# One scatter a unit for tiles 6 to 19, and folds dealt to units without low halves of rows or the transform alone

## The chip, the cores and the metric

The kernel runs on one core of a Trainium2 chip. Its time is the device time of one launch in microseconds (us). The page of the profile names five engines: PE (TensorE, with PEld for its weight loads), DVE (VectorE), ACT (ScalarE), POOL (GpSimd) and SP (SyncE, which here only issues DMAs).

## The reference

```python
X = fft(fft(x, axis=1), axis=2).real          # x: 8 x 3072 x 256
a = x @ w_a; b = x @ w_b                      # x is now 24576 x 256, w_a and w_b 256 x 1536
x = (a * b) @ w_out                           # back to 24576 x 256
e_idx = argmax(x @ w_gate)                    # one of 8 experts for each row
out[row] = gate_w * eom * (relu(x[row] @ w1[e]) @ w2[e])
```

All matrix products run in float16 with each factor split into a high and a low half, and three of the four products of halves summed.

## The kernel before

**Stages.** A batch's x is first folded: the symmetric parts of its rows are added and subtracted, in six pieces c of 128 rows (`fold_items`, L498). A piece takes `fold1` (L515, three POOL instructions) and `fold2` (L524, four, and two more for c above 2). Then the folded x is scaled and split into halves (`hi`, `lo`, L592 to L600), the transform along the sequence is taken with matmuls against tables that are loaded from HBM (`dft_products`, L650), and the two matrices w_a and w_b, already turned by the transform along the feature axis, are applied (`step`, L850).

**Units.** The middle of the program is a list of 327 units (`plan`, L1187), run in order. A unit "B" is one block of 128 of the 1536 inner features for one tile of 1024 rows (24 tiles, three to a batch, 12 units a tile): 12 matmuls of 128x512 (L828), the product a*b on DVE (L834 to L840 and L861), its high half on ACT (L845), its low half on POOL (L847), and two units later 24 matmuls of 128x256 with w_out (`g2`, L888). A unit "D" is one twelfth of the transform for a group of batches, with no block of features beside it; each of the groups 1 to 4 (`GROUPS`, L34) begins with nine of them, and its last three twelfths ride in "B" units.

**After a tile.** `post_items` (L901) takes the 1024 rows that a tile made: their squares, the high halves on ACT (`row_hi`), the low halves on DVE (`row_lo`, L947, one instruction for 128 rows, in units of 2, 3 and 3), eight transposing DMAs (`turn`), the gates (`gate0` to `gate3`, some 15 small DVE instructions), the place of each row in its expert's list (`place`), and eight indirect DMAs (`scatter`, L1048 to L1050), each of which writes 128 rows to the table `rows` in HBM from POOL's queue. A scatter waits until the scatter before it has landed, since both write `rows`. Beside this run the folds of later batches and `expert_items` (L368), which split the experts' weights, with low halves on DVE (`lo1` L412, `lo2` L465).

**Who sets the order.** `deal` (L185) gives each list of items to units: an item goes to the first unit whose `BUDGET` of ACT, DVE, POOL and SP time it still fits. `reserve` (L182) books room. In a unit, `second` (L842) issues ACT's high half, then what the planner put under "pool0", then POOL's low half L847, and after it `run("pool")`; DVE's items come behind L840. Items of `post_items` are dealt first, then those of the folds and of the experts. All engines then work through their queues in that order, waiting on semaphores.

After the units comes a drain, and then the experts' stage (from L1558 on, 83 blocks of 256 rows and 23 of 128), which sorts nothing any more and is bound by PE.

Of the kernel before, what the change touches and what calls it, by code (L numbers as in the profile page):

```python
# [41 lines left out]
def chain_kernel(ctx, tc, x, x384, w_a, w_b, w_out, w_gate, w_og, w1, w2, dft, c16, c32, ids, out):  # L42
# [129 lines left out]
    def run(point):  # L172
# [3 lines left out]
    BUDGET = {  # L176
        "B": {"act": 2.8, "dve": 1.75, "pool": 3.6, "pe": 1.0, "sp": 4.0},
        "D": {"act": 1.8, "dve": 1.8, "pool": 3.2, "pe": 1.0, "sp": 4.0},
    }
# [318 lines left out]
    def fold_items(b, eng):  # L498
# [25 lines left out]
        def fold2(c):  # L524
            def go():
# [5 lines left out]
                eng.tensor_tensor(out=T if c > 2 else F32[:, c, 0, :], in0=A[:, 0, :], in1=A[:, 1, :], op=ALU.add)  # L531
                eng.tensor_tensor(out=F32[:, c, 1, :], in0=A[:, 0, :], in1=A[:, 1, :], op=ALU.subtract)
                if c > 2:
                    eng.tensor_tensor(out=F32[:, c, 0, :], in0=F32[:, c - 3, 0, :], in1=T, op=ALU.subtract)
                    eng.tensor_tensor(out=F32[:, c - 3, 0, :], in0=F32[:, c - 3, 0, :], in1=T, op=ALU.add)
            return go
# [68 lines left out]
        for i, c in enumerate(order):  # L605
            for k, fn in enumerate((fold1(c), fold2(c))):
                if i == 1 and k == 0:
                    t.append((0, [("sp", 1, load384)]))
                due = [norms.popleft()] if i > 3 and norms else []
                nx = [("sp", 1, load(order[i + 1]))] if k == 1 and i < 5 else []  # L610
                t.append((1 + (i == 0 and k == 0), [("pool", 2.1 if k == 0 else 3.6 if c > 2 else 2.2, fn)] + nx + due))
            if i == 1:
# [288 lines left out]
    def post_items(T):  # L901
# [161 lines left out]
        for a, b in ((0, 2), (2, 5), (5, 8)):  # L1063
            if a >= nt:
                continue
            m = min(b, nt) - a
            items.append((0 if last is None and nt > 4 else 1, [("act", 0.4 * m, c(row_hi, a, b)), ("dve", 0.38 * m, c(row_lo, a, b))] + ([("sp", 2, last)] if last else [])))
            last = c(turn, a, b)
# [6 lines left out]
        ]  # L1075
        for w in range(0, nt, 2):
            items.append((1, [("pool0", 1.3, scatter(w))] + ([("pool", 1.3, scatter(w + 1))] if w + 1 < nt else [])))
# [111 lines left out]
    for g, G in enumerate(GROUPS):  # L1189
        if g:  # L1190
            plan += [("D", g, i, i, 9) for i in range(9)]
            reserve(len(plan) - 1, "act", 0)
            reserve(len(plan) - 1, "dve", 0)
# [670 lines left out]
```

## Time and profile before

| | |
|---|---|
| time, median of 3 runs | 3057.61 us (3049.89 to 3060.44) |
| profiled execution | 3049.82 us, span 3048.1 us |
| PE busy in the span | 2873.9 us (94%) |
| DVE busy | 2212.1 us (73%) |
| POOL busy | 1335.4 us (44%) |
| mean granted PE clock | 0.978 |

The span is the time from the first to the last instruction. The window rows cover, in this order, tiles 7, 8, 9 and 10, the start of tile 11, tiles 14, 15 and 16, three units in tile 17, tiles 20 and 21, and the "D" units of groups 3 and 4 with the unit before them. A share of busy time is an average over stages: in the units DVE is nearly as full as PE, in the experts' stage PE alone is full. Times in windows are counted from the start of the span. "idle before" in a row is the time in which the engine did nothing just before, and the name behind the arrow is what ended it. The profiled execution lies at the lower end of the three runs.

### The profile page before, as it was taken

How to read it: one execution, taken by the hardware profiler on the slowest of the kernel's cores; microseconds unless marked ns; L12 is line 12 of the kernel's file. 1: busy time of each engine (PE TensorE's matmuls, PEld its weight loads, DVE VectorE, ACT ScalarE, POOL GpSimd, SP SyncE). 2: the span in 40 equal slices, each digit the busy share in tenths (PEclk: the TensorE clock that was granted, in tenths of full speed). 3: DMA queues.
4: the chain of work that ended last, by engine and by line, in shares of the span. 5: the costliest groups of instructions: out<-in, count | busy, mean ns of one | idle time of the engine just before them, and what ended most of it. 6: DMA issues, size and time to landing. Idle time of an engine off the chain costs nothing.

```text
span 3048.1 us, 62392 instructions
## 1 busy us (share of the span) xinstructions
PE 2873.9 (94%) x24101; PEld 2181.6 (72%) x24101; DVE 2212.1 (73%) x4079; ACT 1313.7 (43%) x2605; POOL 1335.4 (44%) x1083
## 2 busy tenths in 40 slices
PE   6899899989999989999989999989999999999998
PEld 3566666756666756666666666688888888888898
DVE  8678699688999688999677998744555555555556
ACT  4444455545455445455444444432333333333332
POOL 6466587365775455775333544413211111111112
PEclk7899999999999999999999999999999999999999
DMA  6321622541221551221352212373222222222211
GB/s 210 99 61 43 177 69 60 144 108 44 77 76 47 137 119 46 77 72 46 97 128 84 78 50 89 80 193 96 54 52 51 53 51 52 50 53 51 52 45 34
DMA packets 363577, 244.48 MB, mean 80 GB/s; under 512 B 303101, under 2 KB 320669, under 8 KB 362382
## 3 DMA queue, kind: packets, MB, share of 16 engines
q1 hardware_dynamic: 342158, 184.75, 24.3%
q0 software_dynamic: 18816, 51.54, 5.0%
q10 hardware_dynamic: 2304, 4.20, 0.5%
q8 instruction: 188, 3.08, 0.4%
q14 instruction: 111, 0.91, 0.1%
HBM read 106.60 MB, written 70.33 MB: 58 GB/s over the span
## 4 chain that ended last, share of the span: by engine, by line
PE 72%; DVE 13%; issue 7%; DMA 4%; ACT 3%; POOL 0%; DVEq 0%; SPq 0%; POOLq 0%; ACTq 0%
PE s L828 18%; PE y L894 17%; PE g L1611 16%; PE g L1635 15%; PE s L662 3%; DVE EE L861 2%; DVE s L837 2%; DVE rows L947 2%; DVE hf L840 1%; DVE AM L835 1%; DMA big<-in_dft_dram 1%; DMA rows<-rows,di 1%; PE s L962 1%; ACT BP L834 1%; ACT hl L845 1%
## 5 line engine op out<-in xcount | busy, mean ns | idle before, releaser
L828 PE MATMUL s<-big 128*128 128x512 f16 x3456 | 818.9, 387 | 77.0 <-DVE EE L861 69.2
L847 POOL TENSOR_TENSOR hl<-hf,hl 128x1024 f16<-128x1024 f32 x288 | 626.0, 2174 | 562.4 <-ACT hl L845 431.7
L894 PE MATMUL y<-big,hl 128*128 128x256 f16 x6912 | 820.9, 273 | 0.7 <-POOL hl L847 0.5
L894 PEld LDWEIGHTS <-hl 128*128 128x128 f16 x6912 | 672.1, 98 | 150.7 <-issue 10.7
L828 PEld LDWEIGHTS <-big 128*128 128x128 f16 x3456 | 342.7, 99 | 448.6 <-issue 115.6
L1638 POOL DMA_INDIRECT out_dram<-o,di x189 | 192.1, 1017 | 781.6 <-ACT o L1637 521.1
L845 ACT ACTIVATE hl<-hf 128x1024 f16<-128x1024 f32 x288 | 303.9, 1055 | 507.7 <-DVE hf L840 454.1
L1611 PE MATMUL g<-yt,w1t 128*128 128x256 f16 (+1 forms) x4704 | 493.9, 265 | 3.8 <-DVE w1t L1592 3.8
L1635 PE MATMUL g<-w2t,hh 128*128 128x256 f16 x2896 | 479.5, 273 | 0.0
L1611 PEld LDWEIGHTS <-w1t 128*128 128x128 f16 x4704 | 432.5, 98 | 50.9 <-DVE w1t L1592 4.1
L1614 DVE SCALAR_TENSOR_TENSOR hl<-g,hh 128x512 f16<-128x512 f32 x378 | 260.7, 691 | 241.8 <-ACT hh L1613 241.7
L1635 PE MATMUL g<-w2t,hl 128*128 128x256 f16 x1448 | 394.8, 273 | 0.0
L1613 ACT ACTIVATE hh<-g 128x512 f16<-128x512 f32 x378 | 225.3, 597 | 280.0 <-PE g L1611 280.0
L1635 PEld LDWEIGHTS <-hh 128*128 128x128 f16 x3024 | 294.8, 98 | 33.9
L1050 POOL DMA_INDIRECT rows<-rows,di x192 | 192.7, 1004 | 258.7 <-DMA rows<-rows,di 190.2
L836 DVE SCALAR_TENSOR_TENSOR hf<-s,BP 128x512 f32<-128x512 f32 x288 | 198.2, 688 | 109.1 <-ACT BP L834 99.3
L1596 DVE COPY w2t<-big 128x4104 f16 x98 | 120.4, 1229 | 207.9 <-PE g L1635 207.9
L1637 ACT ACTIVATE o<-g,sc 128x256 f32<-128x256 f32 x189 | 89.5, 473 | 406.3 <-PE g L1635 359.7
L835 DVE SCALAR_TENSOR_TENSOR AM<-EE,s 128x512 f32<-128x512 f32 x288 | 195.9, 680 | 29.9 <-PE s L828 27.7
L861 DVE SCALAR_TENSOR_TENSOR EE<-xe,w,s 128x512 f32<-128x512 f32 x288 | 201.4, 740 | 5.1 <-PE s L828 5.1
L861 DVE SCALAR_TENSOR_TENSOR EE<-big,w,s 128x512 f32<-128x512 f32 x288 | 201.5, 741 | 0.0
L837 DVE SCALAR_TENSOR_TENSOR s<-EE,s 128x512 f32<-128x512 f32 x288 | 197.1, 684 | 0.0
(332 smaller groups left out, 3012.4 us busy)
## 6 DMA issues: line engine op xcount, KB each, us to landing
big<-in_x_dram SPq DMA_DIRECT2D x48, 514.0 KB
big<-in_dft_dram SPq DMA_DIRECT2D x60, 384.0 KB
big<-in_moe_w_dram SPq DMA_DIRECT2D x16, 1024.0 KB
wsc<-big SPq DMA_DIRECT2D x32, 512.0 KB
big<-wsc SPq DMA_DIRECT2D x7, 2050.0 KB
big<-in_dft_dram SPq DMA_DIRECT2D x60, 192.0 KB
big<-wsc ACTq DMA_DIRECT2D x16, 256.2 KB
tail<-rows SPq DMA_TRANSPOSE x192
```

Source lines behind the costliest of these rows:

```text
L828: pe.matmul(out=s[ab], lhsT=Wt[:, ab, uv, a, fs], rhs=src[:, h + uv, :], start=(uv == 0 and i == 0), stop=(i == 2), skip_group_check=(uv = ...
L835: dve.scalar_tensor_tensor(out=AM[:, 0, :], in0=EE[:, 0, :], scalar=2.0, in1=a, op0=ALU.mult, op1=ALU.subtract)
L836: dve.scalar_tensor_tensor(out=P["hf"][:, 0, :], in0=a, scalar=CA * CA, in1=BP, op0=ALU.mult, op1=ALU.mult)
L837: dve.scalar_tensor_tensor(out=b, in0=EE[:, 1, :], scalar=2.0, in1=b, op0=ALU.mult, op1=ALU.subtract)
L845: act.activation(out=hl[:, 0], in_=hf, func=ACTF.Copy)
L847: pool.tensor_tensor(out=hl[:, 1], in0=hf, in1=hl[:, 0], op=ALU.subtract)
L861: dve.scalar_tensor_tensor(out=EE[:, ab, :], in0=st_x[T[0]], scalar=w0[:, ab, f:f + 1], in1=s[ab], op0=ALU.mult, op1=ALU.add)
L894: pe.matmul(out=Y[w // 2][:, w % 2, :], lhsT=hl[:, h, pm, 128 * j:128 * j + 128], rhs=wo[:, f, a, :], start=(f == 0 and i == 0 and w % 2 = ...
L1611: pe.matmul(out=ps[:, u, :], lhsT=w[:, a, q, 128 * f:128 * f + 128], rhs=yt[:, 2 * h + q, :], start=(m == 0), stop=(m == 5))
L1613: act.activation(out=hh[:, f0:f0 + nu, :], in_=ps, func=ACTF.Relu)
L1614: dve.scalar_tensor_tensor(out=hl[:, f0:f0 + nu, :], in0=ps, scalar=0.0, in1=hh[:, f0:f0 + nu, :], op0=ALU.max, op1=ALU.subtract)
L1635: pe.matmul(out=ps, lhsT=hx[:, f, ts], rhs=wv[:, a, f, :], start=(m == 0), stop=(m == 3 * NF2 - 1))
```

## The change

Three rules of the planner change, and `fold2` is split. No arithmetic changes. (a) Tiles 6 to 19 deal their eight scatters one to a unit, all under "pool0", where before two shared a unit, one ahead of L847 and one behind it. (b) A new resource "lock" with room 1.0 in each unit: the low halves of rows of tiles 6 and above take 1.0 of it, each part of a fold of batches 4 to 7 takes 0.5, and the nine "D" units of groups 2, 3 and 4 have it booked out. So these folds share no unit with low halves of rows, and neither stands in those "D" units; that also moves the low halves of tiles 11 and 17, which stood there. (c) For batches 4 to 7 the last two instructions of `fold2` become `fold3`, an item of its own, in the same unit where POOL's budget allows.

```diff
     BUDGET = {
-        "B": {"act": 2.8, "dve": 1.75, "pool": 3.6, "pe": 1.0, "sp": 4.0},
-        "D": {"act": 1.8, "dve": 1.8, "pool": 3.2, "pe": 1.0, "sp": 4.0},
+        "B": {"act": 2.8, "dve": 1.75, "pool": 3.6, "pe": 1.0, "sp": 4.0, "lock": 1.0},
+        "D": {"act": 1.8, "dve": 1.8, "pool": 3.2, "pe": 1.0, "sp": 4.0, "lock": 1.0},
...
+                st["T", c] = T
+            return go
+
+        def fold3(c):
+            def go():
+                T = st["T", c]
+                eng.tensor_tensor(out=F32[:, c, 0, :], in0=F32[:, c - 3, 0, :], in1=T, op=ALU.subtract)
+                eng.tensor_tensor(out=F32[:, c - 3, 0, :], in0=F32[:, c - 3, 0, :], in1=T, op=ALU.add)
+            return go
...
-            for k, fn in enumerate((fold1(c), fold2(c))):
+            for k, fn in enumerate((fold1(c), both(c)) if b < 4 else (fold1(c), fold2(c)) + ((fold3(c),) if c > 2 else ())):
...
-                t.append((1 + (i == 0 and k == 0), [("pool", 2.1 if k == 0 else 3.6 if c > 2 else 2.2, fn)] + nx + due))
+                t.append((int(k < 2) + (i == 0 and k == 0), [("pool", (2.1, 2.2 if c < 3 or b > 3 else 3.6, 1.35)[k], fn), ("lock", 0.5 if b > 3 else 0.0, None)] + nx + due))
...
-            items.append((0 if last is None and nt > 4 else 1, [("act", 0.4 * m, c(row_hi, a, b)), ("dve", 0.38 * m, c(row_lo, a, b))] + ([("sp", 2, last)] if last else [])))
+            items.append((0 if last is None and nt > 4 else 1, [("act", 0.4 * m, c(row_hi, a, b)), ("dve", 0.38 * m, c(row_lo, a, b)), ("lock", 1.0 if t > 5 else 0.0, None)] + ([("sp", 2, last)] if last else [])))
...
-        for w in range(0, nt, 2):
+        if 5 < t < NTILE - 4:
+            items += [(1, [("pool0", 1.3, scatter(w))]) for w in range(nt)]
+        for w in range(0, nt if not 5 < t < NTILE - 4 else 0, 2):
             items.append((1, [("pool0", 1.3, scatter(w))] + ([("pool", 1.3, scatter(w + 1))] if w + 1 < nt else [])))
...
             plan += [("D", g, i, i, 9) for i in range(9)]
+            if g > 1:
+                for u in range(len(plan) - 9, len(plan)):
+                    reserve(u, "lock", 1.0)
```

The first place is POOL's queue where tile 7's rows are scattered and tile 8's low halves stand on DVE (units 130 to 134 of the plan). L1050 is a scatter, L847 the low half of a unit's product, L529 to L532 are a `fold2`. Before:

```order
L1050 DMA rows<-rows_100,di 196864x264 x2
L847 TENSOR_TENSOR hl<-hf,hl 128x1024
L1050 DMA rows<-rows_100,di 196864x264
L847 TENSOR_TENSOR hl<-hf,hl 128x1024
L529 TENSOR_TENSOR big<-big 128x2x129
L530 TENSOR_TENSOR big<-big 128x2x127
L531 TENSOR_TENSOR big<-big 128x256
L532 TENSOR_TENSOR big<-big 128x256
```

These are the last three scatters of the tile; the pair at the top is the second scatter of one unit and the first of the next. The fold behind them stands in a unit with three low halves of rows.

With the change the first three scatters of the same tile read so (L1062 is the scatter, L859 the low half of a unit, L519 to L521 a `fold1`, L529 to L532 a `fold2`):

```order
L1062 DMA rows<-rows_100,di 196864x264
L859 TENSOR_TENSOR hl<-hf,hl 128x1024
L519 TENSOR_TENSOR big<-big 128x4x128
L520 TENSOR_TENSOR big<-big 128x4x127
L521 COPY big<-big 128x4
L1062 DMA rows<-rows_100,di 196864x264
L859 TENSOR_TENSOR hl<-hf,hl 128x1024
L529 TENSOR_TENSOR big<-big 128x2x129
L530 TENSOR_TENSOR big<-big 128x2x127
L531 TENSOR_TENSOR big<-big 128x256
L532 TENSOR_TENSOR big<-big 128x256
L1062 DMA rows<-rows_100,di 196864x264
```

No scatter follows another directly any more. In 16 units of the plan one scatter and one part of a fold now stand together; there were none before.

The second place is DVE's queue at the end of the "D" units of group 3. L691 is the low half of a twelfth of the transform, L947 the low halves of tile 11's rows. Before:

```order
L947 SCALAR_TENSOR_TENSOR rows_100<-tail,r_11610,rows_100 128x256 x2
L159 TENSOR_SCALAR pq<-sst 128x2
L160 TENSOR_SCALAR Rt<-pq 128x2
L691 SCALAR_TENSOR_TENSOR big<-s_115,Rt,big 128x256 x2
L159 TENSOR_SCALAR pq<-sst 128x2
L160 TENSOR_SCALAR Rt<-pq 128x2
L691 SCALAR_TENSOR_TENSOR big<-s_116,Rt,big 128x256 x2
L947 SCALAR_TENSOR_TENSOR rows_100<-tail,r_11610,rows_100 128x256 x3
```

All eight instructions of the tile stand in "D" units. With the change the first two come behind the first "B" unit's part of the transform (L703 is the old L691, L873 the old L861, L959 the old L947):

```order
L703 SCALAR_TENSOR_TENSOR big<-s_117,Rt,big 128x256 x2
L873 SCALAR_TENSOR_TENSOR EE<-xe,w_91,s_114 128x512
L873 SCALAR_TENSOR_TENSOR EE<-xe,w_91,s_115 128x512
L159 TENSOR_SCALAR pq<-sst 128x2
L160 TENSOR_SCALAR Rt<-pq 128x2
L703 SCALAR_TENSOR_TENSOR big<-y_118,Rt,big 128x256 x2
L959 SCALAR_TENSOR_TENSOR rows_100<-tail,r_11598,rows_100 128x256 x2
```

Its transposes, gates and scatters move back with it, by four to six units. The same happens to tile 17 in group 4.

## Rows read from the trace of the kernel before

**Rows 1.** The page's first part: each engine's busy us, share of the span, instructions.

```profile
PE 2873.9 (94%) x24101; PEld 2181.6 (72%) x24101; DVE 2212.1 (73%) x4079; ACT 1313.7 (43%) x2605; POOL 1335.4 (44%) x1083
```

**Rows 2.** Windows: start:end, length, busy us of PE, PEld, DVE, ACT, POOL; PEclk; DMA.

```profile
692.40:756.20 63.80, 63.80 (x480) 43.00 (x478) 55.08 (x112) 35.91 (x72) 35.50 (x26) 1.00 0.11 27
756.20:829.10 72.90, 66.55 (x495) 44.23 (x494) 68.23 (x121) 34.80 (x64) 50.42 (x41) 0.95 0.28 81
829.10:897.70 68.60, 66.05 (x498) 44.15 (x497) 63.90 (x119) 38.31 (x73) 56.39 (x50) 1.00 0.29 78
897.70:966.00 68.30, 65.25 (x498) 44.01 (x496) 63.04 (x128) 35.90 (x71) 34.11 (x21) 1.00 0.18 48
992.20:1015.20 23.00, 21.23 (x148) 14.28 (x147) 21.16 (x35) 7.47 (x11) 11.94 (x7) 1.00 0.52 139
1217.10:1289.20 72.10, 67.34 (x496) 44.47 (x494) 65.57 (x122) 34.92 (x64) 49.54 (x41) 0.95 0.29 82
1289.20:1359.10 69.90, 66.08 (x497) 44.01 (x495) 65.33 (x118) 38.20 (x73) 56.05 (x50) 1.00 0.28 77
1359.10:1429.40 70.30, 66.73 (x497) 44.45 (x496) 63.88 (x127) 35.93 (x71) 34.06 (x21) 0.98 0.16 46
1455.70:1475.50 19.80, 17.35 (x110) 10.88 (x109) 17.99 (x28) 6.15 (x9) 10.52 (x6) 0.91 0.44 111
1689.70:1761.20 71.50, 66.81 (x520) 44.93 (x518) 66.59 (x133) 36.48 (x69) 35.44 (x21) 1.00 0.30 83
1761.20:1828.30 67.10, 64.62 (x483) 43.22 (x481) 62.24 (x125) 34.10 (x62) 34.03 (x20) 1.00 0.21 56
1026.60:1079.20 52.60, 47.30 (x407) 37.81 (x406) 26.69 (x68) 30.40 (x91) 24.10 (x27) 1.00 0.73 174
1492.40:1543.40 51.00, 46.30 (x403) 37.35 (x400) 23.71 (x68) 29.45 (x87) 12.27 (x11) 1.00 0.71 174
```

**Rows 3.** Timeline, DVE: start, us, instruction; three low halves in tile 7.

```profile
719.65 1.27 DVE L947 SCALAR_TENSOR_TENSOR rows<-tail,r,rows 128x256 f16<-128x256 f32 x3
```

**Rows 4.** Timeline, DVE and POOL, in tile 8 and where tile 11 begins.

```profile
785.50 7.47 DVE L947 SCALAR_TENSOR_TENSOR rows<-tail,r,rows 128x256 f16<-128x256 f32 x3
...
991.87 0.97 POOL L1050 DMA_INDIRECT rows<-rows,di  x1 [1.83 <-DMA rows<-rows,di]
...
992.85 2.15 POOL L847 TENSOR_TENSOR hl<-hf,hl 128x1024 f16<-128x1024 f32 x1
...
994.10 4.52 DVE L947 SCALAR_TENSOR_TENSOR rows<-tail,r,rows 128x256 f16<-128x256 f32 x3
...
995.17 0.99 POOL L1050 DMA_INDIRECT rows<-rows,di  x1 [0.17 <-issue]
...
996.19 2.14 POOL L847 TENSOR_TENSOR hl<-hf,hl 128x1024 f16<-128x1024 f32 x1
```

**Rows 5.** Groups of instructions, DVE, 692.4 to 1828.3: xcount, busy us, mean ns.

```profile
L947 DVE SCALAR_TENSOR_TENSOR rows<-tail,r,rows 128x256 f16<-128x256 f32 x120 | 89.0, 792 | 0.0
```

**Rows 6.** Source line L1050, its last line, and POOL's waits (us, times, longest).

```profile
DMA to landing us min/median/max: 2.1/2.5/7.2
...
POOL rows L1050 <- DMA rows<-rows,di: 190.2, 77, 6.3
```

**Rows 7.** Windows as in Rows 2: one fold1, one fold2.

```profile
823.42:826.06 2.64, 2.64 (x25) 2.23 (x23) 2.64 (x7) 0.03 (x1) 2.63 (x4) 1.00 0.01 5
829.26:832.14 2.88, 2.88 (x31) 2.18 (x29) 2.78 (x6) 2.13 (x4) 2.71 (x5) 1.00 0.00 0
```

**Rows 8.** Timeline: POOL, a gate's last instruction on DVE, and PE after it.

```profile
648.71 2.12 POOL L847 TENSOR_TENSOR hl<-hf,hl 128x1024 f16<-128x1024 f32 x1
...
648.90 1.96 DVE L1021 TENSOR_TENSOR rows<-g,kt 128x8 f32<-128x8 f32 x1
...
652.11 0.19 PE L1025 MATMUL s<-ohx,c16s 128*128 128x72 f16 x1 [1.61 <-DVE hf L836]
```

**Rows 9.** Timeline, PE, the units of the transform alone in group 3.

```profile
1054.46 8.12 PE L662 MATMUL s<-big 128*128 128x258 f16 x72 [1.31 <-DMA big<-in_dft_dram]
```

More of the change, by code (lines that the diff above doesn't have):

```diff
@@ L532, in go, with both @@
                 eng.tensor_tensor(out=F32[:, c, 1, :], in0=A[:, 0, :], in1=A[:, 1, :], op=ALU.subtract)
+                st["T", c] = T
[6 more added lines that the diff above has]
+            return go
+        def both(c):
+            def go():
+                fold2(c)()
                 if c > 2:
-                    eng.tensor_tensor(out=F32[:, c, 0, :], in0=F32[:, c - 3, 0, :], in1=T, op=ALU.subtract)
-                    eng.tensor_tensor(out=F32[:, c - 3, 0, :], in0=F32[:, c - 3, 0, :], in1=T, op=ALU.add)
+                    fold3(c)()
             return go
```

## The prediction, on record before the run

> **What bounds the kernel now.** I read the page first, then windows tile by tile, then the timeline where a window lost time, then waits and groups for prices. The page says PE is busy for 94% of the span [rows 1], so only PE's idle time and its slow clock can be won. The windows say where that is; "in tile n" means in the window of tile n's twelve units, where the rows of the tile before are worked up. Tile 7's twelve units take 63.80 us with no idle PE at all; DVE is busy 55.08 us of it [rows 2]. Tile 8 takes 72.90 us with PE busy 66.55, tile 10 68.30 with 65.25, tile 14 72.10 with 67.34 [rows 2]. The same loop, so what differs is beside it. The timeline names it: three low halves of rows take DVE 1.27 us in tile 7 [rows 3], 7.47 us in tile 8 and 4.52 us in tile 11 [rows 4]. Over tiles 7 to 21 the 120 of them take a mean of 792 ns [rows 5], against about 1.27 / 3 = 423 ns for one in tile 7. PE then waits for DVE.
>
> Why they are slow can be read in tile 11. A scatter waits 1.83 us for the landing of the one before and starts at 991.87; the unit's POOL half L847 stands behind it and runs only from 992.85; the unit's second scatter follows at 995.17 and the next L847 at 996.19 without a gap [rows 4]. The low halves begin at 994.10 and end at 998.62, which is 0.29 us after that L847 ends at 998.33. So a DVE instruction of this kind waits while POOL works through a backlog. The backlog comes from pairs of scatters: one needs about 1.0 us on POOL and a median of 2.5 us to land [rows 4, 6], so two in a row need 7.0 us, more than a unit of 63.80 / 12 = 5.3 us. In all, scatters waited 190.2 us for landings, 77 times [rows 6].
>
> **The change part by part.** One scatter a unit needs 1.0 + 2.5 = 3.5 us, under 5.3 us, so it has landed before the next is issued; then L847 starts when ACT's half is there, and the low halves pass ahead of it as in tile 7. The idle time of PE in the windows that hold such low halves (length less PE busy [rows 2]): tile 8 6.35, tile 9 2.55, tile 10 3.05, the start of tile 11 1.77, tile 14 4.76, tile 15 3.82, tile 16 3.57, the same place in tile 17 2.45, tile 20 4.69, tile 21 2.48; together 35.5 us. Six of them have no fold beside the low halves (10, 11, 16, 17, 20, 21): 18.0 us. I take 16.9, since about 1.1 us in tile 20 lies at its gates. The other four, 17.5 us, have folds there as well. Tiles 8 and 14 lose 11.1 us, most of it in one unit each, where a fold of 2.64 us [rows 7] comes behind scatter and L847 (the 7.47 us of tile 8); I take all of it. Of tiles 9 and 15, 6.4 us, I take half, since folds stay beside the experts' low halves. That makes 31.2 us.
>
> The clock. In tiles 8 and 14 PE's granted clock has a mean of 0.95, and 0.91 after the low halves at 1455.7, where in tiles 7 and 10 it is 1.00 [rows 2]: a part of these stretches ran at the lower of the two levels after PE had stood idle. PE is busy 1.3, 2.1 and 1.5 us longer in tiles 8, 14 and 16 than in tile 10, with as many matmuls (495 to 498) [rows 2]. I take 4 us back of these 4.9.
>
> The units of the transform alone. What ends PE's waits there is the landing of the tables, with DMA engines 71 to 73% busy and PE idle 5.3 and 4.7 us [rows 2, 9]. A load of x and the transposes of tiles 11 and 17 leave these units, so the tables meet less traffic. Folds there were never what PE waited for: group 4 has none and loses as much. I take 2 us; the ends are 0 and 6.
>
> What the move costs. The low halves of tiles 11 and 17 now stand in units that carry a twelfth of the transform or follow one; at 1.27 us for three they fit as in tile 7, so nothing, as long as no backlog stands on POOL there. Folds: the same instructions, but now in 16 units together with a scatter. Such a unit asks POOL for 0.99 + 2.14 + 2.64 to 2.88 = 5.8 to 6.0 us [rows 4, 7], up to 0.7 us more than 5.3; where two come together the third unit has no fold, so the backlog stays near 1.4 us and the unit's half is consumed two units later. PE waits for nothing there. But a gate or a low half of weights behind a fold can meet L847: a gate's last instruction, 8 elements wide, took 1.96 us beside a L847, and PE stood still 1.61 us in the next unit [rows 8]. By the planner's rules 29 units of groups 2 and 3 follow a fold with such DVE work in before, ten of them with low halves of rows; now there are 37 and none with those. The 19 others now cost about 1.61 for that gate, as much for its like in group 3, and the 3.2 us left in tiles 9 and 15, 6.4 us or 0.34 a unit; 18 more units make 6.1 us. Bounds: 0, since many gates pass in front of L847 untouched, and 18 x 1.61 = 29 us, if each is caught. I take 6.1, by the mean of what such units cost now. `fold3` alone adds no work.
>
> Sum: 31.2 + 4 + 2 - 6.1 = 31.1 us, so 3049.8 - 31 = 3019 us against the profiled execution. That one lies 7.8 us under the median of the runs, so I put the same gain against the median: 3057.6 - 31.1 = 3026.5, say 3026 us.
>
> [...]
>
> **The rivals.**
> First: a single scatter is enough to hold low halves of rows up. For it: at the start of tile 11 the three together overlap a scatter and two L847 [rows 4]. Against it: the end of the wait is that of the second L847 (998.33), not that of the scatter (996.16); it is the L847 without a gap behind the scatter that held on. If it holds, the 16.9 us stay, tiles 7, 13 and 18, clean so far, lose about 2.5 us each like tile 21 [rows 2], and half of the clock comes back: 14.3 + 2 + 2 - 6.1 - 7.5 = 4.7 us of gain, 3053 us.
>
> Second: folds find other victims. The pairs' 16.9 us go, but what tiles 8, 9, 14 and 15 win (14.3 us) is paid again at gates and weights' halves. Then 16.9 + 2 + 2 - 6.1 = 14.8 us, 3043 us. For it: each part of a fold costs POOL 2.6 to 2.9 us [rows 7], two for each of 24 pieces in four batches, and DVE has 55 to 68 us of work in a tile [rows 2]. Against it: in tile 9 POOL is busy 56.39 of 68.60 us with six parts of folds, and PE idles 2.55 us only [rows 2].
>
> Third, slower: POOL becomes the bound in the stretches where a scatter and a fold share units. If the backlog of up to 0.7 us a unit is not worked off and L847 has no gap ahead of it, each of the 37 units behind a fold loses what the gate lost, 1.61 us: 59.6 us against the 37.2 that the rest brings, so 22 us slower, 3080 us. It decides from 23 caught units on (37.2 / 1.61). Against it: POOL is 44% busy overall [rows 1], and fullest in tile 9.
>
> That the low halves are not what PE waits for can't be, with tile 7 beside tile 8.
>
> **How the numbers follow.** The forecast has a chance of 0.62, the folds' other victims 0.21, the single scatter 0.09, the slower case 0.05, and 0.03 is for a gain that is larger than the sum by all of the tables' waits. The forecast's own spread is 3012 to 3040: 35.5 us, 4.9 of clock and 6 of tables gone with no new stalls would give 46 us, 3011; with twice the new stalls it is 24 us, 3033, and the profiled execution's lower place allows some 5 us below. The second rival's 3043 lies inside a range up to 3047. So 3008 to 3047. A time within 0.3% (9 us) is no change that runs of this kernel can tell. Faster: 0.62 + 0.21 + 0.03, less a little for cases that end short of 9 us: 0.85. Same: 0.09. Slower: 0.06.
>
> **What would show it.** In the changed profile the mean of the low halves of rows over tiles 7 to 21 falls from 792 ns to 450 to 550; scatters' waits for landings fall by more than half from 190.2 us; PE's idle time in tiles 10, 16 and 21 falls under 1 us, and the granted clock in tile 14 is 0.98 or more. If low halves stay at 700 ns or more with single scatters beside them, the first rival is right. If they are quick, but DVE's gates and experts' halves show instructions of 1.5 us and more and PE idles there, it is the second; if POOL shows no gaps over whole tiles and PE waits for L847's line or for gates in every tile, the third. Wrong would be any time over 3047 us.

## The result, and the profile after the change

| | before | after |
|---|---|---|
| median of the runs | 3059.03 us (4 runs, 3049.89 to 3060.81) | 3009.12 us (4 runs, 3008.65 to 3010.20) |
| profiled execution | 3049.82 us | 3008.71 us |
| span | 3048.1 us | 3006.9 us |
| PE busy in the span | 2873.9 us | 2863.5 us |
| mean granted PE clock | 0.978 | 0.983 |

The ratio after to before is 0.9843, 95% interval 0.9823 to 0.9864: faster by 1.6%. The forecast was 3026 us with a range of 3008 to 3047, so the side and the range hold and the gain is larger than its sum. Profile against profile it is 41.1 us where 31.1 were worked out; the medians lie 50 us apart, since before's profiled execution lies at the foot of its runs.

The windows of after that answer to [rows 2], in the same order: tiles 7, 8, 9, 10, the same place in tile 11, tiles 14, 15, 16, the same place in 17, tiles 20, 21, and the "D" units of groups 3 and 4. Columns as there.

```profile
689.10:753.60 64.50, 64.50 (x487) 43.62 (x485) 56.99 (x114) 37.81 (x75) 43.77 (x35) 1.00 0.14 38
753.60:819.60 66.00, 65.87 (x511) 44.66 (x509) 60.59 (x121) 36.29 (x68) 42.40 (x32) 1.00 0.29 77
819.60:884.90 65.30, 64.77 (x482) 43.25 (x480) 60.39 (x118) 35.04 (x67) 53.26 (x46) 1.00 0.32 90
884.90:950.60 65.70, 65.17 (x498) 44.02 (x497) 59.56 (x124) 35.33 (x71) 43.84 (x34) 1.00 0.20 50
976.80:997.70 20.90, 20.90 (x147) 14.15 (x145) 20.36 (x38) 10.18 (x15) 12.60 (x9) 1.00 0.55 152
1197.70:1265.80 68.10, 65.20 (x503) 44.18 (x500) 65.22 (x123) 36.00 (x68) 45.64 (x36) 1.00 0.24 56
1265.80:1332.20 66.40, 66.40 (x484) 44.13 (x483) 58.12 (x117) 34.28 (x64) 49.78 (x42) 0.98 0.32 93
1332.20:1398.70 66.50, 64.89 (x495) 43.72 (x493) 62.27 (x123) 37.68 (x75) 43.37 (x34) 1.00 0.25 73
1425.10:1446.00 20.90, 20.90 (x147) 14.14 (x145) 20.61 (x40) 10.30 (x16) 12.66 (x9) 1.00 0.48 128
1650.40:1718.60 68.20, 65.64 (x515) 44.52 (x513) 64.26 (x138) 35.10 (x69) 36.29 (x22) 1.00 0.24 68
1718.60:1789.00 70.40, 67.76 (x500) 44.89 (x499) 62.95 (x122) 35.29 (x64) 34.96 (x21) 0.98 0.26 72
1009.30:1058.90 49.60, 46.88 (x407) 37.97 (x406) 21.17 (x59) 26.42 (x80) 14.88 (x14) 1.00 0.72 184
1457.60:1506.50 48.90, 46.90 (x407) 37.83 (x405) 20.85 (x61) 26.42 (x80) 12.32 (x11) 1.00 0.72 180
```

Length less PE busy is PE's idle time. In tile 8 it falls from 6.35 to 0.13 us, in tile 10 from 3.05 to 0.53, in tile 15 to nothing. Tiles 14 (2.90), 16 (1.61), 20 (2.56) and 21 (2.64) still have some, and tile 21 is longer than before, 70.40 for 67.10.

The low halves of rows in the same stretch of tiles 7 to 21 (DVE group, columns as in [rows 5]) and POOL's waits for a landing over the whole span (as in [rows 6]):

```profile
L959 DVE SCALAR_TENSOR_TENSOR rows<-tail,r,rows 128x256 f16<-128x256 f32 x120 | 53.9, 502 | 0.0
```

```profile
POOL rows L1062 <- DMA rows<-rows,di: 158.7, 57, 6.0
```

The mean falls from 792 to 502 ns. The same place as in [rows 4], now in tile 8: the timeline of POOL and DVE.

```profile
780.28 0.99 POOL L1062 DMA_INDIRECT rows<-rows,di  x1 [0.16 <-issue]
781.88 1.27 DVE L959 SCALAR_TENSOR_TENSOR rows<-tail,r,rows 128x256 f16<-128x256 f32 x3
783.21 2.19 POOL L859 TENSOR_TENSOR hl<-hf,hl 128x1024 f16<-128x1024 f32 x1 [1.93 <-ACT hl L857]
```

The scatter waits for no landing and is done at 781.27. L859 waits for ACT's half, and the three low halves pass in that gap, 1.27 us as in [rows 3]. In [rows 4] the 7.47 us of the three in tile 8 end 0.3 us behind the fold part L520, when three POOL instructions have run without a gap:

```profile
788.11 2.14 POOL L847 TENSOR_TENSOR hl<-hf,hl 128x1024 f16<-128x1024 f32 x1
790.19 1.28 POOL L519 TENSOR_TENSOR big<-big 128x512 f32<-128x512 f32 x1
791.41 1.26 POOL L520 TENSOR_TENSOR big<-big 128x508 f32<-128x508 f32 x1
```

Where the 41.1 us lie, by the starts of the units in both traces (the start of a unit is that of its first L861 on DVE, L873 after the change): 1.4 in the tiles up to 6, 6.9 in the three stretches of "D" units that changed (1.9, 2.9 and 2.1), 31.0 in the twelve-unit tiles 7 to 21, minus 1.2 in tiles 22 and 23, and 3.0 behind the last unit. Of PE's idle time that is left in tiles 7 to 21, 27.8 us with the "D" units, waits ended by DVE are 23.2. In tile 20 one of DVE's other instructions meets L859:

```profile
1692.94 0.99 POOL L1062 DMA_INDIRECT rows<-rows,di  x1 [0.16 <-issue]
...
1700.21 0.97 POOL L1062 DMA_INDIRECT rows<-big,di  x1 [6.28 <-DVE m L996]
...
1700.64 5.33 DVE L465 SCALAR_TENSOR_TENSOR big<-big,r2e 128x512 f16<-128x512 f32 x1 [0.17 <-ACT big L459]
1701.19 4.22 POOL L859 TENSOR_TENSOR hl<-hf,hl 128x1024 f16<-128x1024 f32 x2
...
1707.23 0.59 PE L829 MATMUL s<-big,ones 1*128 1x512 f16 x2 [2.56 <-DVE hf L848]
```

The scatter of a one-row tile at the end of the sequence (`rows<-big`) still shared a unit with another scatter. It waited 6.28 us at the head of POOL's queue, two L859 then ran without a gap, and an expert's low half that takes 0.74 us elsewhere took 5.33. The row names a DVE instruction, but what it had waited for is the landing of the scatter of 1692.94. That scatter landed at 1699.4. The DMA issues of 1690 to 1703 (KB each where the bytes are fixed, then median us to landing) show what else moved at the time:

```profile
big<-in_moe_w_dram SPq DMA_DIRECT2D x1, 1024.0 KB
...
rows<-rows,di POOLq DMA_INDIRECT x1, 6.5
```

A load of an expert's weights of 1024 KB is among them, and the scatter's 6.5 us compare with a median of 2.5 [rows 6]. That the load delayed it was not tested by itself.

### The profile page after: what moved, and what is told of

It reads as the page before. It is cut to its first block, busy times and chain, and to the rows that moved or that the text cites. A ratio compares the mean times of both kernels' runs of the same rounds, so it can differ in the third digit from the quotient of the medians.

```text
span 3006.9 us, 62393 instructions
## 1 busy us (share of the span) xinstructions
PE 2863.5 (95%) x24101; PEld 2181.8 (73%) x24101; DVE 2169.6 (72%) x4079; ACT 1312.5 (44%) x2605; POOL 1335.9 (44%) x1083
## 4 chain that ended last, share of the span: by engine, by line
PE 79%; DVE 10%; issue 5%; DMA 3%; ACT 2%; SPq 0%; POOL 0%; DVEq 0%; POOLq 0%; ACTq 0%
PE y L906 21%; PE s L840 20%; PE g L1628 16%; PE g L1652 16%; PE s L674 3%; DVE EE L873 2%; DVE s L849 1%; DMA big<-in_dft_dram 1%; DMA rows<-rows,di 1%; PE s L974 1%; DVE hf L852 1%; DVE AM L847 1%; DVE rows L959 1%; ACT big L702 1%; DVE big L703 0%
## 5 line engine op out<-in xcount | busy, mean ns | idle before, releaser
L859 POOL TENSOR_TENSOR hl<-hf,hl 128x1024 f16<-128x1024 f32 x288 | 629.4, 2186 | 580.0 <-ACT hl L857 500.4
L840 PE MATMUL s<-big 128*128 128x512 f16 x3456 | 810.5, 384 | 51.4 <-DVE EE L873 46.9
L1062 POOL DMA_INDIRECT rows<-rows,di x192 | 191.3, 996 | 200.0 <-DMA rows<-rows,di 158.7
L847 DVE SCALAR_TENSOR_TENSOR AM<-EE,s 128x512 f32<-128x512 f32 x288 | 196.2, 681 | 36.3 <-PE s L840 34.6
L873 DVE SCALAR_TENSOR_TENSOR EE<-xe,w,s 128x512 f32<-128x512 f32 x288 | 201.6, 741 | 5.1 <-PE s L840 5.1
L873 DVE SCALAR_TENSOR_TENSOR EE<-big,w,s 128x512 f32<-128x512 f32 x288 | 201.6, 742 | 0.0
```

The source lines that it names most:

```text
L840: pe.matmul(out=s[ab], lhsT=Wt[:, ab, uv, a, fs], rhs=src[:, h + uv, :], start=(uv == 0 and i == 0), stop=(i == 2), skip_group_check=(uv = ...
L847: dve.scalar_tensor_tensor(out=AM[:, 0, :], in0=EE[:, 0, :], scalar=2.0, in1=a, op0=ALU.mult, op1=ALU.subtract)
L859: pool.tensor_tensor(out=hl[:, 1], in0=hf, in1=hl[:, 0], op=ALU.subtract)
L873: dve.scalar_tensor_tensor(out=EE[:, ab, :], in0=st_x[T[0]], scalar=w0[:, ab, f:f + 1], in1=s[ab], op0=ALU.mult, op1=ALU.add)
```

## The experiments

Each was timed beside the kernel before on the same chip, in three sessions (medians of before 3055.5 to 3057.0), so versions are best compared by their ratios to before. In the texts on record a mean of 449 ns for the changed kernel is the group's busy time by its count; the row's own mean is 502. This table holds the lengths of windows in us, by the starts of units (up to 0.1 us from the rounded windows above), to which the parts below refer; "end" is from the start of the last unit to the end of the span.

| window | before | after | e1_scatter | e2_lock | e3_nod | e9_wide |
|---|---|---|---|---|---|---|
| tile 8 | 72.9 | 66.0 | 70.0 | 72.5 | 64.6 | 66.6 |
| tile 9 | 68.5 | 65.3 | 67.7 | 69.2 | 65.5 | 64.8 |
| tile 10 | 68.3 | 65.7 | 67.3 | 70.8 | 65.7 | 65.7 |
| tile 14 | 72.1 | 68.1 | 66.0 | 73.3 | 66.9 | 66.6 |
| tile 15 | 70.0 | 66.4 | 69.4 | 70.9 | 64.8 | 64.8 |
| tile 16 | 70.3 | 66.5 | 67.0 | 71.4 | 66.2 | 66.1 |
| tile 20 | 71.5 | 68.2 | 68.1 | 70.6 | 66.8 | 67.0 |
| tile 21 | 67.1 | 70.4 | 64.3 | 73.8 | 64.3 | 64.3 |
| "D", group 3 | 52.6 | 49.6 | 52.6 | 49.4 | 52.6 | 52.1 |
| "D", group 4 | 51.0 | 48.9 | 50.9 | 49.9 | 51.0 | 51.0 |
| start of the last unit | 1961.2 | 1923.1 | 1929.0 | 1968.6 | 1915.4 | 1906.8 |
| end | 1086.9 | 1083.9 | 1087.0 | 1084.0 | 1091.0 | 1091.0 |

**Part (a) alone, e1_scatter.** The kernel before with this edit:

```diff
-        for w in range(0, nt, 2):
+        if 5 < t < NTILE - 4:
+            items += [(1, [("pool0", 1.3, scatter(w))]) for w in range(nt)]
+        for w in range(0, nt if not 5 < t < NTILE - 4 else 0, 2):
             items.append((1, [("pool0", 1.3, scatter(w))] + ([("pool", 1.3, scatter(w + 1))] if w + 1 < nt else [])))
```

> The kernel before with part (a) alone: one scatter a unit for tiles 6 to 19; folds, lock and fold3 as before. My theory: a low half of a row waits when POOL works without a gap, and pairs of scatters make such stretches. Then the tiles without folds beside their low halves (10, 11, 16, 17, 20, 21) lose their waits; in the profile after the change these windows together gained 12 us. In tiles 8, 9, 14 and 15 low halves still share units with folds, so a half of their 17.7 us stays. That is 12 + 9 = 21 us off 3059: 3038, and the mean of the low halves over tiles 7 to 21 is about 580 ns (792 before, 449 after). Rival: the folds alone hold the low halves up and the pairs only happen to stand near them. Then the mean stays above 700 ns and the time is 3050 or more.

Measured: 3017.51 us, ratio 0.9869 (0.9852 to 0.9886). 39.5 us of gain where 21 were expected, and the low halves are as quick as in the changed kernel although folds still stand in their units:

```profile
L947 DVE SCALAR_TENSOR_TENSOR rows<-tail,r,rows 128x256 f16<-128x256 f32 x120 | 52.7, 490 | 0.0
```

The rival is out, and so is my own share for the folds: three of these 120 took over 560 ns, the longest 979, so a fold with no pair near it hardly holds low halves of rows up. What parts (b) and (c) still add is less sure: the medians lie 8 us apart, but the intervals of the two ratios overlap. In the traces the last unit starts 5.9 us later here than in the changed kernel: tiles 8, 9 and 15 are 9.3 us longer, the "D" stretches of groups 3 and 4 by 4.9, tiles 14 and 21 shorter by 8.2.

**Parts (b) and (c) alone, e2_lock.** The changed kernel with the edit above undone.

> The changed kernel with its scatters in pairs again: lock, units of the transform alone kept free, and fold3 stay. My theory: low halves beside pairs of scatters stay slow in tiles 10, 11, 16, 17, 20 and 21 (12 us), and tiles 8 and 14 gain only what the folds cost, about 9 us; the stretches of the transform alone keep their 7 us. That is 16 to 20 us off 3059: 3041, with a mean of the low halves of about 650 ns. The two parts then add up to the whole (21 + 18 = 39 of 50 us, the rest between them). Rival: keeping folds away is what frees the low halves. Then the time is within 10 us of the changed kernel's 3009 and the mean under 550 ns.

Measured: 3058.50 us, ratio 1.0009 (0.9999 to 1.0019). Nothing is gained; my theory said 16 to 20 us. The mean of the low halves is 826 ns. Tile 10 of this kernel has no fold near its low halves, and its timeline shows the whole mechanism:

```profile
921.42 0.99 POOL L1062 DMA_INDIRECT rows<-rows,di  x1 [0.17 <-issue]
...
924.22 0.98 POOL L1062 DMA_INDIRECT rows<-rows,di  x1 [1.80 <-DMA rows<-rows,di]
925.21 2.15 POOL L859 TENSOR_TENSOR hl<-hf,hl 128x1024 f16<-128x1024 f32 x1
...
925.94 5.04 DVE L959 SCALAR_TENSOR_TENSOR rows<-tail,r,rows 128x256 f16<-128x256 f32 x3
...
927.53 0.99 POOL L1062 DMA_INDIRECT rows<-rows,di  x1 [0.17 <-issue]
928.55 2.14 POOL L859 TENSOR_TENSOR hl<-hf,hl 128x1024 f16<-128x1024 f32 x1
...
934.15 2.29 PE L840 MATMUL s<-big 128*128 128x512 f16 x5 [3.12 <-DVE EE L873]
```

A scatter waits 1.80 us for a landing, so L859 starts late, at 925.21, when DVE comes to the low halves. They wait for its end (927.36), go on beside the next scatter, and the last of them meets the next L859 and waits until 930.69. PE then stands still for 3.12 us. So the two parts do not add up as I had written: keeping folds away is worth nothing while the pairs are there, and some 8 us at most, not clear of noise, once they are gone.

**Without the rule on "D" units, e3_nod.**

```diff
-            if g > 1:
-                for u in range(len(plan) - 9, len(plan)):
-                    reserve(u, "lock", 1.0)
```

> The changed kernel without the third rule: the units of the transform alone may hold low halves of rows and folds again. The prediction's step says 2 us for keeping them free; the profile after the change shows the three stretches 1.9, 2.9 and 2.1 us shorter, 7 us in all. If low halves, transposes and the load of x in these units were what held the tables up, they get longer again by 7 us and the time is 3016. Rival: the stretches got shorter since the scatters and the rows that they write left them or are spread; then they stay at 52.2, 49.6 and 48.9 us and the time is 3009 within 3 us.

Measured: 3007.00 us (3006.56 to 3010.86), ratio 0.9836 (0.9821 to 0.9851). Both theories have a half: the stretches of groups 3 and 4 are as long again as before (52.6 and 51.0), so the rule did shorten them, by 3.0 and 2.1 us; and the time is no longer, because tiles 14, 15, 20 and 21 come out 1.2, 1.6, 1.4 and 6.1 us shorter when gates, folds and experts' halves are dealt otherwise. That dealing did this is argued from the table, not tested. In the sum the rule shows no gain.

**No fold in the unit before low halves, e6_reach.**

```diff
                 reserve(u, p.rstrip("0"), c)
+                if p == "lock" and c == 1.0:
+                    reserve(u - 1, p, 0.6)
```

> The changed kernel with one more rule: low halves of rows also take room of the lock in the unit ahead of theirs, so that no part of a fold stands in the unit before low halves. It moves the folds of one batch in tiles 12 and 13 by one unit to three. In the changed kernel's trace one group of low halves of tiles 7 to 21 is still slow, 3.89 us for three at 1081.07, with a fold of the unit before still running on POOL; PE waits 1.98 and 2.14 us around it. My theory: these 4 us go, 3005, and the mean of the low halves over tiles 7 to 21 is 480 ns. Rival: the folds that move catch other instructions of DVE and the time stays at 3009 within 2 us.

Measured: 3014.05 us (3003.63 to 3018.28), ratio 0.9851 (0.9831 to 0.9870). The slow group at 1081 is gone, but another low half took 3.03 us at 1290, and the last unit starts at 1923.3 as in the changed kernel (1923.1); its end took 1090.5 us for 1083.9. In this run the move brought nothing, and the spread of 15 us is wider than what was to be told apart: inconclusive on the 4 us, and it shows that a time of this kernel is not settled by the units alone.

**What on POOL holds a low half up, e4_memset and e5_tt.** Both put five POOL instructions on a tile of their own into the gap in which the low halves pass; they add work and leave nothing out.

```diff
+        def extra():
+            for _ in range(5):
+                pool.memset(dum, 1.0)                                           # e4_memset
+                pool.tensor_tensor(out=dum, in0=dum, in1=dum, op=ALU.mult)      # e5_tt
...
-            items.append((0 if last is None and nt > 4 else 1, [("act", 0.4 * m, c(row_hi, a, b)), ("dve", 0.38 * m, c(row_lo, a, b)), ("lock", 1.0 if t > 5 else 0.0, None)] + ([("sp", 2, last)] if last else [])))
+            items.append((0 if last is None and nt > 4 else 1, [("act", 0.4 * m, c(row_hi, a, b)), ("dve", 0.38 * m, c(row_lo, a, b)), ("lock", 1.0 if t > 5 else 0.0, None)] + ([("pool0", 0.0, extra)] if 5 < t < NTILE - 3 else []) + ([("sp", 2, last)] if last else [])))
```

Each version has one of the two marked lines; "..." stands for lines left out here, among them the tile `dum` of 128x128 f32 and a memset of it at the start.

> The changed kernel with added work that computes nothing: in each unit with low halves of rows of tiles 6 to 20, five POOL memsets of a tile of 128x128 f32 behind the unit's scatter and ahead of its low half L859 on POOL. POOL is then busy while the low halves start on DVE, but reads no SBUF. There the changed kernel's trace leaves POOL idle for 1.8 to 1.9 us. Theory 1: low halves wait only for POOL instructions that read SBUF. Then they stay at a mean of 449 to 480 ns and the time stays at 3009, 3012 at most. Theory 2: any POOL instruction that is running or queued holds them up. Then each of 45 units loses about 1 us for the memsets and up to 3 us where a low half then meets L859: 3055 to 3140.

> The same place and count as the memsets, but five POOL tensor_tensor multiplications of that 128x128 tile by itself, about 0.32 us each by the fold's 0.64 us for 128x256. Both theories: the low halves wait for the last of the five or for the gap between two, and then meet L859. Each of 45 units loses 1 to 3 us: 3055 to 3140, with a mean of the low halves over 700 ns. [...]

Measured: with memsets 3009.12 us, ratio 0.9850 (0.9826 to 0.9873), mean of the low halves 484 ns. With multiplications 3014.66 us, ratio 0.9868 (0.9853 to 0.9883), mean 575 ns. First the memsets' timeline, then the multiplications' (in both L961 is the low half of rows, L861 that of a unit, L966 the added instruction):

```profile
785.52 1.27 POOL L966 MEMSET dum<- 128x128 f32 x5
...
786.07 1.27 DVE L961 SCALAR_TENSOR_TENSOR rows<-tail,r,rows 128x256 f16<-128x256 f32 x3
...
787.38 2.13 POOL L861 TENSOR_TENSOR hl<-hf,hl 128x1024 f16<-128x1024 f32 x1 [0.59 <-ACT hl L859]
```

```profile
778.42 1.55 DVE L961 SCALAR_TENSOR_TENSOR rows<-tail,r,rows 128x256 f16<-128x256 f32 x3
...
778.61 2.57 POOL L966 TENSOR_TENSOR dum<-dum 128x128 f32<-128x128 f32 x5
```

Memsets beside the low halves cost nothing. Multiplications cost a low half a wait for one of them (616 ns is its usual duration there) and no more: each multiplication waits for the one before it and leaves a gap of 78 ns, and DVE gets its turn there. POOL waits a little as well: the multiplications of the row take 0.46 and 0.53 us beside low halves and 0.40 alone (0.32 were reckoned). That is theory 1 for the memsets. The multiplications stayed under both figures of the second text: 3014.66 us for 3055 to 3140, and a mean of 575 ns for over 700.

The thirteen traces of this study hold 2496 low halves of rows. 1597 overlap no POOL instruction: 462 to 490 ns. 60 began beside a memset: 471 to 488 ns. 405 began beside a running scatter: 329 of them took 462 to 487 ns, and behind the start of each of the other 76 a POOL tensor instruction began within 0.69 us, directly behind the scatter. 258 began beside a POOL tensor instruction with more than 0.26 us still to run: 255 took over 560 ns. The others began in the last 0.26 us of a POOL instruction or met one later.

A low half does not always wait for one instruction only. Where POOL's next tensor instruction leaves a gap of 78 or 79 ns (85 places) DVE got in every time. Where it leaves none DVE got in 70 times, but 12 times an instruction on DVE (a low half of rows or of an expert) was held through the next one as well, always ahead of L519, L520 or another L847: so in tile 8 of before, 7.47 us, where it was L847, L519 and L520 in a row, and in tile 20 above, 5.33 us, with two L859. What decides it where POOL leaves no gap, no run here shows.

This explains most of the 3.0 us that the traces show again and again: a scatter leaves 1.19 us between two L847 of a backlog (995.00 to 996.19 in [rows 4], 927.36 to 928.55 in e2_lock; the text of e10_twos has 1.03 for it; 1.02 is the time from the scatter's start to that L847), low halves follow each other by 0.40 us, so two get through and the third, which starts some 0.57 us ahead of the next L847, is held by it (0.57 to 0.58 us at all nine low halves of 3.0 us in the profile of before). Alone, at 0.48 us, it would have ended 0.1 us before that L847's row begins; from these two numbers I estimate that POOL's hold reaches some way ahead of the row, and by how much was not measured.

**Pairs in every second unit, e8_pairs2.**

```diff
-            items += [(1, [("pool0", 1.3, scatter(w))]) for w in range(nt)]
+            items += [(2 - (w == 0), [("pool0", 1.3, scatter(w)), ("pool", 1.3, scatter(w + 1))]) for w in range(0, nt, 2)]
```

> The changed kernel with its scatters of tiles 6 to 19 in pairs again, one before and one behind L859, but in every second unit, so eight in eight units as in the changed kernel. Theory 1: what hurts is the rate. A pair in each of four units in a row makes a scatter wait for the landing of the one before, at the head of POOL's queue, and L859 behind it starts late; a pair with an empty unit behind it lands in time. Then low halves stay quick (mean under 520 ns) and the time is 3009 to 3014. Theory 2: two scatters in one unit as such make the backlog. Then about half of the low halves' units are caught, the mean is about 620 ns and the time 3025 to 3033.

Measured: 3017.41 us (3012.94 to 3018.26), ratio 0.9869 (0.9854 to 0.9884). By the low halves theory 1 is right: a mean of 499 ns, and the last unit starts at 1922.9, as in the changed kernel. For the low halves the rate does the harm, not the pair. The median is 8 us longer all the same (the intervals of the two ratios overlap), and the profile puts that behind the last unit: the end takes 1093.6 us for 1083.9, with the same instructions. Whether the pairs have a part in that is open.

**Low halves in units of two, with the pairs, e10_twos.** The kernel before with

```diff
-        for a, b in ((0, 2), (2, 5), (5, 8)):
+        for a, b in ((0, 2), (2, 4), (4, 6), (6, 8)) if 5 < t < NTILE - 1 else ((0, 2), (2, 5), (5, 8)):
```

> The kernel before with one size changed: the low halves of rows of tiles 6 to 22 stand in four units of two each, where they stood in units of 2, 3 and 3. Scatters stay in pairs and folds are not locked. Theory from the traces so far: after a pair's scatter L847 starts about 1.03 us after the L847 before it has ended. Low halves that waited for that end start a new one every 0.4 us, so two pass in the gap and the third meets the next L847: in ten traces every low half of 3.0 us is one that starts some 570 ns ahead of an L847. With two in a unit the 3.0 us go, the first one's wait of about 1.2 us stays: mean over tiles 7 to 21 about 550 to 600 ns (792 before) and, since an expert's low half is the third one in some units, 20 us rather than 32 of gain: 3037. Rival: the order of POOL's work alone decides and a low half waits whenever a pair is near; then the mean stays above 700 ns and the time is 3050 or more.

Measured: 3064.29 us, ratio 1.0016 (1.0001 to 1.0031). On the low halves the theory holds in part: in tiles 7 to 21 none takes 3.0 us any more, and the mean falls to 680 ns. On the time it is wrong. Taking for each kind of DVE instruction the time over its tenth percentile, tiles 7 to 21 of before lose 38.5 us in low halves of rows and 44.6 in all others; here 24.9 and 69.7. With a backlog on POOL, what is spared in one DVE instruction is lost in the next. (In the changed kernel the two are 3.1 and 42.9; in e1_scatter, where folds are not kept apart, 2.0 and some 55.)

**A version from these runs, e9_wide, and two variations.** The changed kernel without the "D" rule and with

```diff
-        if 5 < t < NTILE - 4:
+        if 2 < t < 21:
...
-        for w in range(0, nt if not 5 < t < NTILE - 4 else 0, 2):
-            items.append((1, [("pool0", 1.3, scatter(w))] + ([("pool", 1.3, scatter(w + 1))] if w + 1 < nt else [])))
+        for w in range(0, nt if not 2 < t < 21 else 0, 2):
+            items.append((1, [("pool0", 1.3 if nt > 1 else 3.0, scatter(w))] + ([("pool", 1.3, scatter(w + 1))] if w + 1 < nt else [])))
```

> A version made from what the runs show: the changed kernel without the rule on the units of the transform alone, with single scatters for tiles 3 to 20 and the scatter of the one-row tile at the end kept out of units with another scatter. In the changed kernel's trace low halves beside pairs in tiles 3 to 5 and 22 still take up to 3.0 us each (PE waits of 1.6, 2.6, 3.2 and 3.1 us), and a wait of 6.28 us of that one scatter at 1700 costs PE 2.6 us. Theory: the version without the rule is at 3007.0, and about 10 us of these go: 2997. Rival: the folds of the first batches move with the scatters and catch other instructions of DVE; then it stays at 3007 within 3 us.

Measured: 2996.94 us (2995.18 to 2999.63), ratio to before 0.9804 (0.9791 to 0.9818). It beats both kernels; the interval of its ratio lies just below the changed kernel's (0.9823 to 0.9864). The windows of its tiles 21 and 22:

```profile
1714.20:1778.40 64.20, 64.15 (x481) 43.18 (x480) 59.10 (x124) 34.08 (x62) 34.36 (x20) 1.00 0.20 59
1778.40:1843.20 64.80, 64.80 (x496) 43.91 (x495) 57.57 (x121) 34.57 (x64) 33.97 (x21) 1.00 0.25 71
```

e11_wide_d puts the "D" rule of e3_nod's diff back, e12_wide_twos deals low halves by twos with the diff of e10_twos.

> The version with single scatters for tiles 3 to 20 (2996.9 in the runs), with the rule on the units of the transform alone put back. The rule shortened three of these stretches by 2 to 3 us each in the changed kernel, and the tiles after them gave it back. Theory 1: what came back there are accidents of where gates and experts' halves then stand; on average nothing is gained: 2997 to 3000. Theory 2: the rule's 7 us show here: 2990.

> The version with single scatters for tiles 3 to 20, with low halves of rows in units of two as well, for tiles 6 to 22. If single scatters have freed the low halves already, twos add nothing but a unit of delay for a tile's transposes and gates: 2995 to 3001. If the third low half is still the one that meets L859 in places, some 5 us go: 2991.

Measured: 3002.16 us (2994.06 to 3006.98), ratio 0.9817 (0.9793 to 0.9840), and 3004.80 us (3000.91 to 3011.06), ratio 0.9837 (0.9815 to 0.9860). Neither helps. With the rule the "D" stretches are 51.0 and 49.0 us, 1 to 2 shorter, and tile 21 is at 70.4 again; theory 1 is nearer, its time missed by 2 us. By twos the low halves have a mean of 477 ns and the time is longer than either text said, perhaps because the work that follows a tile's rows comes a unit later and meets other things; no run shows that.

## Why the prediction was right, point by point

**What bounds the kernel.** Right. PE stands idle for 58.0 us from tile 7 to tile 21 of before, the "D" units among them; waits that DVE ended are 44.9 of these, and none is a wait for POOL's half. The longest row of PE's waits there:

```profile
PE s L828 <- DVE EE L861: 40.4, 21, 6.4
```

In e1_scatter, with low halves at 490 ns, the idle time is 34.1 us, the waits for DVE 20.0, and the time 39.5 us shorter.

**The pairs.** The step "it has landed before the next is issued" holds in the "B" units and fails in the "D" units: waits for landings while tiles 8 to 19 run fall from 86.2 us in 36 waits to 48.4 in 14, and these 14 all stand in the "D" units of groups 3 and 4, where scatters take 3.1 to 6.1 us to land and not 2.5. Over the whole span they fall from 190.2 to 158.7 only, where I had asked for less than half: the other 104 us of before, now 110, belong to tiles whose pairs stay or to the drain, and I had not split the row by stage. Of the 16.9 us for tiles 10, 11, 16, 17, 20 and 21, five gave 15.7 (2.6, 1.9, 3.8, 4.1 and 3.3) and tile 21 gave back 3.3, by the next point.

**Folds.** The total for tiles 8, 9, 14 and 15 came out near, in part by luck: 17.7 us, against 14.3 and most of the 4 of the clock (tiles 8 and 14 run at 1.00 now, [rows 2] had 0.95; the lower of the two levels is 0.50, granted in tile 8 of before from 792.8 to 799.4, with PE idle since 789.8). The reason was half wrong. "A fold comes behind scatter and L847; I take all of it" gave the fold the blame. Without touching the folds e1_scatter has 10.5 of the 17.7; with the folds alone e2_lock has nothing. The backlog of the pairs was the cause, and the fold made it longer: 2.4 us of the 7.47 in tile 8 are L519 and L520.

**New stalls, minus 6.1.** Mis-sized, and by the wrong count. DVE's instructions other than low halves of rows take 42.9 us over their quick times now (counted as in e10_twos), 44.6 before; the folds found about as many victims as they had, not more. But where they stand decides a tile. The place that "none with those" excluded exists: a fold of the unit before reaches over into low halves.

```profile
1080.75 1.27 POOL L520 TENSOR_TENSOR big<-big 128x508 f32<-128x508 f32 x1
1081.07 3.89 DVE L959 SCALAR_TENSOR_TENSOR rows<-tail,r,rows 128x256 f16<-128x256 f32 x3
...
1082.38 2.30 POOL L859 TENSOR_TENSOR hl<-hf,hl 128x1024 f16<-128x1024 f32 x1
```

And tile 21 lost its gain to an expert's low half that began together with L859 and took 2.69 us for 0.74; PE then waited 1.98 us:

```profile
1721.82 2.69 DVE L465 SCALAR_TENSOR_TENSOR big<-big,r2e 128x512 f16<-128x512 f32 x1
1721.85 2.12 POOL L859 TENSOR_TENSOR hl<-hf,hl 128x1024 f16<-128x1024 f32 x1 [2.95 <-ACT hl L857]
```

**"D" units.** Mis-sized: 2 us, measured 2.9 and 2.1 in groups 3 and 4 and 1.9 in group 2. e3_nod shows for groups 3 and 4 that the rule is the cause, and that the whole gains nothing by it.

**The sum.** For the tiles it was 31.2 + 4 - 6.1 = 29.1, and the tiles gave 31.0: 12.4 and 17.7 as above, and 0.9 in the five tiles that had no term. So near it came by terms that missed in both directions. Over the same stretch, two of the "D" stretches included, PE lost 30.2 us of idle time and 5.8 of busy time (mean granted clock 0.986 before, 0.994 after), where 4 were taken for the clock. The "D" units gave 5 more than their 2; the tiles before 7 and after 21 made 0.2, and the stage behind the last unit 3.0, which the sum had no term for. That stage has the same number of instructions in eleven of the thirteen traces, and a few more in the two with units of two. It takes 1083.9 to 1093.6 us, and PE's longest wait in it, for the drain, 7.9 to 11.9. So one profile against another can be off by up to 10 us there; with one trace a kernel it stays open whether that is chance or comes of how the units end. Two figures of the prediction's spread are loose: with twice the new stalls the sum gives 25.0 us of gain, not 24, and the bounds worked out, 3011 and 3033, are not those stated, 3012 and 3040.

**The anchor.** I set the gain of 31.1 against the median of 3057.6, 7.8 over the profiled execution, in the belief that after would spread likewise. After's four runs lie within 1.6 us and its profiled one at their foot (3008.71). That is 7 of the 17 us by which the forecast was high; 10 are the terms above. What was longer in before's other runs has no trace.

**The rivals.** First, the single scatter: refuted by e1_scatter and by the 329 quick low halves beside scatters; at 781.88 above the scatter had already ended, so that place is no test of it. Second, folds' other victims: in the sum false. DVE's instructions do still meet POOL in tiles 12, 20 and 21, but in tiles 20 and 21 it is L859 that holds an expert's low half, not a fold. Third, POOL as the bound: POOL is busy 35 to 53 us in the tiles' windows of 64 to 70; not seen. Of the signs, the mean of the low halves (502, in 450 to 550), the clock in tile 14 (1.00) and the idle time in tile 10 (0.53) came as written; tiles 16 and 21 missed "under 1 us", and the waits for landings did not fall by half.

## What to carry to other kernels

Look for the instruction that makes a queue late, not for those that suffer: here eight indirect DMAs that wait for one another's landing, two to a unit, shifted POOL's own work by 1.8 us ([rows 4], e2_lock) into DVE's, and spacing them brought 39.5 of some 50 us, while moving the victims away brought nothing before that was done (e2_lock, e10_twos), and afterwards little that is clear of noise by the lock and nothing by units of two (e12_wide_twos). An instruction that is slow in one version and quick in the next says little while the queue that stops it is still late: what was spared there was lost in the next instruction (e10_twos). Before a gain is set against a median, see whether the profiled run is a typical one.

## What the runs showed of the hardware that was not expected

POOL's memsets and scatters leave DVE's low halves alone (471 to 488 ns beside memsets, 462 to 487 beside scatters); POOL's tensor instructions hold them up (255 of the 258 that began beside one with more than 0.26 us to run took over 560 ns). A low half goes on in a gap of 78 or 79 ns between two of these (85 of 85 places), and sometimes, but not always, where one follows the other without a gap (70 of 82 places).

An instruction with a single tensor input can be stopped as well, here for 1.75 us. In e1_scatter, on 8 elements a partition:

```profile
814.79 2.13 POOL L847 TENSOR_TENSOR hl<-hf,hl 128x1024 f16<-128x1024 f32 x1
814.95 0.22 DVE L1003 TENSOR_REDUCE gs<-go 128x8 f32<-128x64 f32 x1
815.20 1.75 DVE L1007 TENSOR_SCALAR gs<-gs 128x8 f32<-128x8 f32 x1
```

The reduction passes beside L847 at its usual 0.22 us; the one behind it, usually 0.17, ends at 816.95, as L847 does (816.92). In the thirteen traces all 27 of this `tensor_scalar` on 8 elements that began between 600 and 1900 us beside a POOL tensor instruction of over 1 us with more than 0.4 us to run were held, and one on a single element was not (153 ns). None of 76 reductions from SBUF was held (161 to 220 ns for the nine in before and after), nor any of 6484 `scalar_tensor_tensor` of a unit's products, which have one input in SBUF and one in PSUM (668 to 748 ns for the 966 in before and after). What tells those that wait from those that do not, no run here shows.
